# The branch to a fallback path, moved ahead of the last sums and stores of a two-stage kernel

## Chip, cores, metric

The kernel runs on one core of one Trainium2 chip. The metric is the device time of one execution in microseconds, as the median of several runs. The core has five engines with instruction streams of their own: TensorE (PE, and PEld for its weight loads), VectorE (DVE), ScalarE (ACT), GpSimd (POOL) and SyncE (SP), which here only starts transfers.

## What is computed

Two stages follow each other: a gated linear recurrence for each of 4 x 8 heads, and a bilinear feed-forward layer over the 3072 tokens that come out of it.

```python
f = 1 / (1 + exp(-f_logit))                      # q, k, v, f_logit: (4, 8, 768, 48)
for t in range(768):
    state = f[:, :, t, :, None] * state + k[:, :, t] (x) v[:, :, t]   # 48 x 48 for each head
    y[:, :, t] = q[:, :, t] @ state
x = y.transpose(0, 2, 1, 3).reshape(3072, 384)
out = ((x @ w_a) * (x @ w_b)) @ w_out            # w_a, w_b: (384, 1536), w_out: (1536, 384)
```

## The kernel before

There are two complete ways to the output in one program. `by_quotients` is the fast one. It divides running products of the gates by each other, which holds only while the decays stay within a range. `by_levels` is general and slower. The fast way always runs. On the way it gathers evidence on the range (`tails`, `held`), near its end `sum_held` and `check_held` (L915 to L927) turn it into one integer `bad`, and after it the program reads `bad` (`values_load`, L129) and branches (L130): if it is set, `convert_again` and `by_levels` do all the work once more, else nothing is left to do. With the inputs of the reference it is not set. A `values_load` is an instruction on each of the five engines (TENSOR_LOAD in the profile), and so is the branch (COMPARE_BRANCH). On the side that is not taken, each engine adds to its semaphores what the other side would have added: these are the EVENT_SEMAPHORE rows of L130. The end block, with the line of the launch, L1619, waits for every semaphore on SyncE and then brings all engines together.

The fast way works in 8 blocks of 384 tokens. The recurrence of a block (scores, masked products, carried state) comes in two units of four heads. Its result goes by DMA into `xT`, the layer's input with channels on partitions. The up products of blocks 0 and 1 are plain (`up_steps`, L593). Those of the other six use a scheme with 15 products of half size in place of 18 (`up_triples`, products L715, sums L707), with sums of weights made beforehand in `combine_w_ba`. The products with `w_out` (`down`, from L790) take two groups of 128 tokens at a time and use a scheme with 7 block products in place of 8. Each block product is six matmuls of 128x192 outputs (L808).

The order of work is made at build time. `main` (from L1103) is the list of TensorE's steps, with the copies and sums that belong to them standing behind the product that they follow; other work (`lines`, L1145) is fitted in by a planner with costs and due times, `fill` at L1236. At the end of `main` only steps of `down` for the last pair of groups are left, and the instructions stand in the order in which `down` yields them. That order, for this pair, is

1. products `x0` (L849), ACT copies it to `u2` (L823)
2. products `m1` (L854), ACT copies them into half of `o1` (L830)
3. products added to `x0` (L856), ACT copies it into half of `o0` (L834); a sum for `s4` on VectorE (L859)
4. products `x1` (L860), then `sum_u2` and `sum_u3` on VectorE (L837, L840)
5. products `m0` (L863), then `last_of(1, 1, m0)`, a sum on VectorE (L843)
6. products added to `x1` (L865), then `last_of(1, 0, x1)` and `store(1)` (L847), a DMA of 128 x 384 numbers that SyncE starts
7. products added to `m0` (L868), then `last_of(0, 1, m0)` and `store(0)`

`u2`, `o1` and `o0` are tiles from rotating pools, in SBUF; `x0`, `m1`, `x1` and `m0` are the four banks `ps_f` in PSUM.

Of the kernel before, what the change touches and what calls it, by code (L numbers as in the profile page):

```python
# [12 lines left out]
FP32 = mybir.dt.float32  # L13
# [9 lines left out]
BLK = 384  # L23
# [74 lines left out]
@with_exitstack  # L98
def kernel(
    ctx: ExitStack,  # L100
    tc: tile.TileContext,
    q: bass.AP,
    k: bass.AP,
    f_logit: bass.AP,
    v: bass.AP,
    masks: bass.AP,
    moe_w_a: bass.AP,
    moe_w_b: bass.AP,
    moe_w_out: bass.AP,
    out: bass.AP,  # L110
):
    nc = tc.nc
    DFF, DM = moe_w_out.shape[0], out.shape[1]
    NKT, NFT = DM // 128, DFF // 128

    const = ctx.enter_context(tc.tile_pool(name="const", bufs=1))

    def fixed(shape, name, dtype=FP32):
        return const.tile(shape, dtype, tag=name, name=name)

    ident = fixed([128, 128], "ident")
    w_ba = fixed([128, 2, NKT, DFF], "w_ba")
    w_out = fixed([128, NFT, DM], "w_out")
    bad = fixed([1, 1], "bad", I32)
    weights = (w_ba, w_out)

    with ExitStack() as pools:
        by_quotients(pools, tc, q, k, f_logit, v, moe_w_a, moe_w_b, moe_w_out, out, ident, weights, bad)
    again = nc.values_load(bad[0:1, 0:1], min_val=0, max_val=1, skip_runtime_bounds_check_because="it is a comparison's result")  # L129
    with tc.If(again > 0):  # L130
        with ExitStack() as pools:
            convert_again(pools, tc, weight_pieces(*weights, moe_w_a, moe_w_b, moe_w_out))
        with ExitStack() as pools:
            by_levels(pools, tc, q, k, f_logit, v, masks, out, ident, weights)


def by_quotients(ctx, tc, q, k, f_logit, v, moe_w_a, moe_w_b, moe_w_out, out, ident, weights, bad):
    nc = tc.nc
    B, H, D, S = q.shape
    w_ba, w_out = weights  # L140
# [207 lines left out]
            yield  # L348

    ps_x, ps_y = (ps_a.tile([128, 2, 512], FP32, tag=n, name=n) for n in ("ps_x", "ps_y"))  # L350
    ps_f = [ps_a.tile([128, 512], FP32, tag=f"ps_f{i}", name=f"ps_f{i}") for i in range(4)]
    idle = list(range(4))

    def tokens(n, c, p):
# [221 lines left out]
    def on(engine, load, due, do, *args, copied=False):  # L576
        return engine + COPIED * copied, load, beats[0] + due if due else 1 << 30, do, *args
# [209 lines left out]

    down_first = [thirds[0]]

    def down(pair):  # L790

        b11, b21, b22 = (w_out[:, HFT * i:HFT * i + HFT, HM * j:HM * j + HM] for i, j in ((0, 0), (1, 0), (1, 1)))
        t1, t2, t3, t4 = combos
        (blk0, g0), (blk1, g1) = pair
        a11, a12 = (half_of(products(blk0)[:, g0], i) for i in range(2))
        a21, a22 = (half_of(products(blk1)[:, g1], i) for i in range(2))
        got = {}

        def block():
            down_first[0] = thirds[(thirds.index(down_first[0]) + 1) % 3]  # L800
            return thirds[thirds.index(down_first[0]) - 1].rearrange("p (k j t) -> p k j t", k=NI, j=2)

        def add(due, to, x, y, op=ALU.add):
            return on(DVE, 880, due, add_steps, to, x, y, op)

        def emit(to, x, w, start, i):
            for i in (i, i + 1):
                nc.tensor.matmul(  # L808
                    to, lhsT=x[:, i // 2, i % 2], rhs=w[:, NI * (i % 2) + i // 2],
                    start=start and i == 0, stop=i == HFT - 1, skip_group_check=True,  # L810
                )

        def times(to, x, w, start=False):
            for i in range(0, HFT, 2):
                yield on_pe(BEAT, emit, to, x, w, start, i)

        s3 = block()
        yield add(4, s3, a11, a21, ALU.subtract)
        x0, m1, x1, m0 = (ps_f[i][:, 0:HM] for i in free)

        def begin():
            got["u2"] = sb2.tile([128, HM], FP32, tag="u2", name="u2")
            nc.scalar.copy(got["u2"], x0)  # L823

        def part(i, j):
            return got["o", i][:, HM * j:HM * j + HM]

        def second():
            got["o", 1] = sb1.tile([128, DM], FP32, tag="o1", name="o1")
            nc.scalar.copy(part(1, 0), m1)  # L830

        def third():
            got["o", 0] = sb1.tile([128, DM], FP32, tag="o0", name="o0")
            nc.scalar.copy(part(0, 0), x0)  # L834

        def sum_u2():
            nc.vector.tensor_tensor(got["u2"], x1, got["u2"], ALU.add)  # L837

        def sum_u3():
            nc.vector.tensor_tensor(part(1, 0), got["u2"], part(1, 0), ALU.add)  # L840

        def last_of(i, j, x):
            nc.vector.tensor_tensor(part(i, j), x, got["u2"] if i == 0 else part(1, 0), ALU.add)  # L843

        def store(i):
            blk, g = pair[i]
            nc.sync.dma_start(out=out[blk * BLK + g * 128:blk * BLK + g * 128 + 128], in_=got["o", i])  # L847

        yield from times(x0, a11, b11, True)  # L849
        yield on(ACT, 220, 4, begin)  # L850
        s1, s2 = block(), block()
        yield add(10, s1, a21, a22)
        yield add(7, s2, s1, a11, ALU.subtract)
        yield from times(m1, s3, t3, True)  # L854
        yield on(ACT, 220, 7, second)
        yield from times(x0, a12, b21)  # L856
        yield on(ACT, 220, 7, third)
        s4 = block()
        yield add(10, s4, a12, s2, ALU.subtract)  # L859
        yield from times(x1, s2, t2, True)  # L860
        yield on(DVE, 270, 4, sum_u2)
        yield on(DVE, 270, 0, sum_u3)
        yield from times(m0, s1, t1, True)  # L863
        yield on(DVE, 270, 4, last_of, 1, 1, m0)
        yield from times(x1, a22, t4, True)  # L865
        yield on(DVE, 270, 8, last_of, 1, 0, x1)
        yield on(SP, ISSUE, 3, store, 1)
        yield from times(m0, s4, b22)  # L868
        yield on(DVE, 270, 4, last_of, 0, 1, m0)
        yield on(SP, ISSUE, 3, store, 0)  # L870

    def core_parts(s):

# [49 lines left out]
    def check_held():  # L923

        ps = ps_x[0:1, 0, 0:1]
        nc.tensor.matmul(ps, lhsT=some[:, 0:1], rhs=ones, start=True, stop=True)
        nc.vector.tensor_scalar(bad, ps, 128.0 * NU * 3, None, ALU.is_lt)  # L927

    def patterns():
        make_identity(nc, ident)  # L930
# [7 lines left out]
    with tc.manual_schedule():  # L938
# [161 lines left out]


        w_out_sums, (w_before, w_over) = list(combine_w_out()), combine_w_ba()
        main, beside, behind = [], {}, {}  # L1103
        for blk, i in ups[alone:]:
            main.extend(up_steps(blk, i))
            main.append(on(DVE, 480, 2, product))
# [2 lines left out]
        for blk in range(NBLK):  # L1109
            if blk >= 2:  # L1110
                beside[len(main)] = "x", blk
                main.extend(up_triples(blk))
                behind[blk] = len(main)
                ahead = 16
            b, odd = divmod(blk, 2)
            pairs = (((blk - 1, 0), (blk, 0)), ((blk, 1), (blk, 2))) if odd else (((blk, 1), (blk, 2)),)
            if blk == 1:
                pairs = (((0, 1), (0, 2)), *pairs)
            for two in pairs if blk else ():
                beside.setdefault(len(main), "out")  # L1120
                first, *steps = down(two)
                at = len(main) - ahead
                main.insert(at, first)
                beside = {n + (n > at): x for n, x in beside.items()}
                if blk == NBLK - 1 and two is pairs[0]:
                    steps.insert(0, on(DVE, 700, 0, sum_held))
                    steps.append(on(PE, 100, 0, check_held))
                main.extend(steps)
                behind.setdefault("down", len(main))
                ahead = 10  # L1130
# [141 lines left out]
        done = len(main)  # L1272
        for line in lines:
            emit_until(line, len(line.steps))


def by_levels(ctx, tc, q, k, f_logit, v, masks, out, ident, weights):


    nc = tc.nc  # L1280
# [13 lines left out]
    sb2 = ctx.enter_context(tc.tile_pool(name="sb2", bufs=2))  # L1294
    ab_pool = ctx.enter_context(tc.tile_pool(name="ab", bufs=NFT + 2))
    ps_a = ctx.enter_context(tc.tile_pool(name="ps_a", bufs=2, space=bass.MemoryType.PSUM))
    ps_f = ctx.enter_context(tc.tile_pool(name="ps_f", bufs=4, space=bass.MemoryType.PSUM))

    def fixed(shape, name):
        return fixedp.tile(shape, FP32, tag=name, name=name)  # L1300
# [219 lines left out]
    def ffn(b):  # L1520

        x = xT.pop(b)
        for blk in range(NB):
            cols = slice(blk * BLK, blk * BLK + BLK)
            ab = []
            for ft in range(NFT):
                ps = {}
                for nm, w in (("b", w_b), ("a", w_a)):
                    ps[nm] = ps_f.tile([128, 512], FP32, tag="f", name="f")[:, 0:BLK]
                    for kt in range(NKT):  # L1530
                        nc.tensor.matmul(
                            ps[nm],
# [8 lines left out]
                nc.vector.tensor_tensor(ab[ft], ps["a"], b_sb, ALU.mult)  # L1541
                yield
            for tg in range(NTG):
                o = ps_f.tile([128, 512], FP32, tag="f", name="f")[:, 0:DM]
                for ft in range(NFT):
                    y = ab[ft][:, tg * 128:tg * 128 + 128]
                    nc.tensor.matmul(o, lhsT=y, rhs=w_out[:, ft], start=ft == 0, stop=ft == NFT - 1)
# [75 lines left out]
```

## Time and profile before

| | |
|---|---|
| median of 3 runs | 598.5 us (598.17 to 599.41) |
| profiled execution | 597.91 us |
| its span, from the first to the last instruction | 596.2 us |
| mean granted clock of TensorE | 0.997 |
| chain that ended last, share of the span | PE 84%, DVE 10%, issue 2%, ACT 1%, DMA 1% |

The profile is of one execution. The 1.7 us between its time and its span lie outside the instructions. In rows of groups, "x12" counts instructions, and "mean ns" is the time of one. In the timeline each row is a start, a length, the engine and line, output <- input, and in brackets the idle time ahead of it with what ended it. A q behind an engine's name (SPq, PEldq) means its sequencer: reads of registers, branches, waits on semaphores and DMA issues, which do not count as busy. In views by line, three durations are the shortest, median and longest, and then come the first and last start. The page's chain ends like this in the order of time (start, length, what):

```profile
569.88 6.01 PE ps_f L808 x37
575.89 0.12 PE ps_x L926 x2
576.01 13.86 PE ps_f L808 x84
589.87 0.02 issue
589.89 0.36 DVE o L843
```

It ends with the last sum. What the program does after that (stores, reads of the flag, branches, waits) is sequencer work, which this chain does not follow.

### The profile page before, as it was taken

Reading aid. Unit: us, or ns where it says so; the run is one execution under the profiler, and the core shown is the slowest. Engines: PE = TensorE matmul, PEld = TensorE weight load, DVE = VectorE, ACT = ScalarE, POOL = GpSimd, SP = SyncE. Lnnn points to the kernel's source line nnn. Section 1 sums busy time; section 2 is a strip of 40 time slices with the busy share of each in tenths; the row PEclk is TensorE's granted clock in tenths of the full one; section 3 lists DMA queues with packets and bytes.
Section 4 is the critical chain, followed back from the end, with each engine's and each line's share of the span. In section 5 each row is a group of like instructions: output and inputs, shape, how many; then the busy total and the mean of one; then the engine's idle time right before and its main releaser. Section 6 shows DMA issues by size and latency. Waiting matters only on the chain.

```text
span 596.2 us, 13953 instructions
## 1 busy us (share of the span) xinstructions
PE 571.8 (96%) x5802; PEld 512.0 (86%) x5802; DVE 412.3 (69%) x786; ACT 269.3 (45%) x507; POOL 77.0 (13%) x71
## 2 busy tenths in 40 slices
PE   3899999999999999999999999999999999999995
PEld 1655655567999999999999999999999999999995
DVE  6899445599977778958895677838784256745741
ACT  6589959743123464245521354325431345144300
POOL 6254525354000000000000000000000000000000
PEclk9999999999999999999999999999999999999998
DMA  8697699099542440044004400050001100000000
GB/s 215 184 257 226 211 252 263 0 157 186 118 134 66 113 100 3 17 120 93 2 2 128 117 10 1 2 127 21 3 1 47 48 1 0 2 27 1 0 30 32
DMA packets 33273, 49.43 MB, mean 83 GB/s; under 512 B 3952, under 2 KB 24976, under 8 KB 33200
## 3 DMA queue, kind: packets, MB, share of 16 engines
q1 hardware_dynamic: 30000, 42.38, 26.0%
q0 software_dynamic: 3056, 5.92, 5.8%
q8 instruction: 47, 0.77, 0.6%
q14 instruction: 26, 0.21, 0.1%
q10 hardware_dynamic: 144, 0.15, 0.1%
HBM read 33.23 MB, written 4.72 MB: 64 GB/s over the span
## 4 chain that ended last, share of the span: by engine, by line
PE 84%; DVE 10%; issue 2%; ACT 1%; DMA 1%; SPq 0%; DVEq 0%; ACTq 0%
PE ps_f L715 35%; PE ps_f L808 28%; PE ps_f L593 13%; PE ps_y L484 2%; DVE inv L329 2%; PE ps_y L510 2%; PE ps_x L387 2%; PE ps_x L435 1%; PE ps_x L411 1%; DVE sums L707 1%; DVE groups L707 1%; DVE spare L329 1%; DVE f_in L316 1%; DVE q_in L333 1%; DVE w_ba L73 1%
## 5 line engine op out<-in xcount | busy, mean ns | idle before, releaser
L593 PE MATMUL ps_f<-xT,w_ba 128*128 128x384 f32 x288 | 95.6, 489 | 1.9 <-DMA xT<-y 1.4
L1271 ACT COPY sums<-ps_f 128x384 f32<-128x384 f32 x120 | 57.5, 480 | 75.9 <-PE ps_f L715 68.2
L593 PEld LDWEIGHTS ps_f<-xT,w_ba 128*128 128x128 f32 x288 | 53.9, 190 | 38.6 <-issue 2.6
L1271 ACT COPY groups<-ps_f 128x384 f32<-128x384 f32 x120 | 57.7, 481 | 62.9 <-PE ps_f L715 39.9
L715 PE MATMUL ps_f<-xT,w_ba 128*128 128x192 f32 x384 | 78.4, 327 | 0.0
L715 PEld LDWEIGHTS ps_f<-xT,w_ba 128*128 128x128 f32 x384 | 64.7, 190 | 0.2
L715 PE MATMUL ps_f<-groups,w_ba 128*128 128x192 f32 x288 | 55.5, 328 | 0.0
L715 PE MATMUL ps_f<-x_sums,raw 128*128 128x192 f32 x288 | 54.0, 331 | 1.2 <-DVE groups L707 0.9
L808 PE MATMUL ps_f<-w_out,sums 128*128 128x192 f32 x288 | 52.2, 329 | 0.3 <-DVE groups L615 0.3
L808 PE MATMUL ps_f<-w_out,groups 128*128 128x192 f32 x288 | 51.7, 328 | 0.0
L715 PEld LDWEIGHTS ps_f<-x_sums,raw 128*128 128x128 f32 x288 | 46.9, 190 | 4.3 <-DVE groups L707 1.8
L808 PE MATMUL ps_f<-spare,sums 128*128 128x192 f32 x288 | 49.0, 326 | 0.0
L715 PEld LDWEIGHTS ps_f<-groups,w_ba 128*128 128x128 f32 x288 | 47.8, 190 | 0.5 <-ACT groups L1271 0.3
L808 PEld LDWEIGHTS ps_f<-w_out,sums 128*128 128x128 f32 x288 | 47.1, 190 | 1.3 <-DVE groups L615 0.6
L808 PEld LDWEIGHTS ps_f<-w_out,groups 128*128 128x128 f32 x288 | 47.1, 190 | 0.7
L312 POOL TENSOR_SCALAR inv<-inv 128x768 f32<-128x768 f32 x14 | 13.1, 935 | 267.3 <-ACT inv L309 267.2
L808 PEld LDWEIGHTS ps_f<-spare,sums 128*128 128x128 f32 x288 | 47.1, 190 | 0.1
L60 POOL TENSOR_SCALAR sums<-sums 128x768 f32<-128x768 f32 (+1 forms) x20 | 39.7, 1983 | 45.0 <-ACT sums L58 44.8
L707 DVE TENSOR_TENSOR sums<-sums,groups 128x768 f32<-128x768 f32 x36 | 34.7, 965 | 14.2 <-ACT groups L1271 13.7
L707 DVE TENSOR_TENSOR sums<-ps_f,sums 128x384 f32<-128x384 f32 x60 | 32.9, 553 | 16.5 <-PE ps_f L715 15.0
L715 PE MATMUL ps_f<-x_sums,w_ba 128*128 128x192 f32 x192 | 39.3, 327 | 0.5 <-DVE sums L707 0.5
L715 PE MATMUL ps_f<-xT,raw 128*128 128x192 f32 x192 | 39.4, 328 | 0.0
(136 smaller groups left out, 868.0 us busy)
## 6 DMA issues: line engine op xcount, KB each, us to landing
raw<-w_ba POOLq DMA_DIRECT2D x11, 512.0 KB, 8.5
k_in<-in_k_dram SPq DMA_DIRECT2D x32, 144.0 KB, 3.8
q_in<-in_q_dram SPq DMA_DIRECT2D x32, 144.0 KB, 4.2
v_in<-in_v_dram SPq DMA_DIRECT2D x16, 288.0 KB, 5.4
raw<-in_moe_w_out_dram SPq DMA_DIRECT2D x6, 768.0 KB, 6.3
out_dram<-o SPq DMA_DIRECT2D x24, 192.0 KB, 1.9
f_in<-in_f_logit_dram SPq DMA_DIRECT2D x28, 144.0 KB, 2.9
xT<-y SPq DMA_DIRECT2D x45, 72.0 KB, 2.2
```

Source lines behind the costliest of these rows:

```text
L60: nc.gpsimd.tensor_scalar(h, h, HI_MAX, None, ALU.min)
L73: nc.vector.tensor_tensor(dst[:, rows], hu[:, rows], bit[:, rows], ALU.add)
L312: nc.gpsimd.tensor_scalar(inv, inv, EXP_K, 1.0, ALU.mult, ALU.add)
L329: nc.vector.tensor_tensor_scan(inv[:, w], inv[:, w], none[:, 0:C], first, ALU.mult, ALU.add)
L387: nc.tensor.matmul(ps[h][SUB * p:SUB * p + SUB, o:o + SUB], lhsT=kf[r, tokens(n, c, p)], rhs=qf[r, tokens(n, c, p)], start=True, stop=True,)
L484: nc.tensor.matmul(ps[p][e:e + D, o:o + SUB], lhsT=t["v"][r, n, c, h * D:h * D + D], rhs=at[r, h, o:o + SUB], start=o == 0, stop=True, ski ...
L510: nc.tensor.matmul(ps[p][e:e + D, o:o + SUB], lhsT=st[j][r, n], rhs=qf[r, tokens(n, c, p)], start=False, stop=True, skip_group_check=True,)
L593: nc.tensor.matmul(ps[nm][:, 0:BLK], lhsT=w[:, kt, ft * 128:ft * 128 + 128], rhs=xT[blk][:, kt], start=kt == 0, stop=kt == NKT - 1,)
L707: nc.vector.tensor_tensor(to, x, y, op)
L715: nc.tensor.matmul(ps[:, g], lhsT=sums_of_w[name][:, g, 128 * j:128 * j + 128], rhs=sums_of_x[blk][name], start=start and g == 0, stop=Tru ...
L808: nc.tensor.matmul(to, lhsT=x[:, i // 2, i % 2], rhs=w[:, NI * (i % 2) + i // 2], start=start and i == 0, stop=i == HFT - 1, skip_group_ch ...
L1271: do(*args)
```

## The change

The last two sums (`last_of(1, 0, x1)` and `last_of(0, 1, m0)`) and the two stores behind them leave the common stream. `down` puts them on a list, `ending`, and the program emits them in the other arm of the branch, so that they run when the flag is not set; if it is set, the general path writes all of the output, these rows too. The read of the flag moves into `down`, behind the sum for `s4` and ahead of the products `x1`, as a step of SyncE with a cost of 600 ns for the planner; as before it is an instruction on all five engines. The branch stands behind the last products on TensorE, behind `last_of(1, 1, m0)` on VectorE, behind the copy of `o0` on ACT, behind the read on SyncE and POOL. In this last pair `u2`, `o1` and `o0` lie in parts of `w_ba`, since the pools of the fast way are closed where the other arm begins. The four banks `ps_f` come from a pool of the whole program for the same reason, and `by_levels` uses them in rotation.

```diff
+    ps_f = ctx.enter_context(tc.tile_pool(name="ps_f", bufs=1, space=bass.MemoryType.PSUM))
+    banks = [ps_f.tile([128, 512], FP32, tag=f"ps_f{i}", name=f"ps_f{i}") for i in range(4)]
 
     with ExitStack() as pools:
-        by_quotients(pools, tc, q, k, f_logit, v, moe_w_a, moe_w_b, moe_w_out, out, ident, weights, bad)
-    again = nc.values_load(bad[0:1, 0:1], min_val=0, max_val=1, skip_runtime_bounds_check_because="it is a comparison's result")
-    with tc.If(again > 0):
+        again, ending = by_quotients(pools, tc, q, k, f_logit, v, moe_w_a, moe_w_b, moe_w_out, out, ident, weights, bad, banks)
+    with tc.If(again > 0) as general:
         with ExitStack() as pools:
             convert_again(pools, tc, weight_pieces(*weights, moe_w_a, moe_w_b, moe_w_out))
         with ExitStack() as pools:
-            by_levels(pools, tc, q, k, f_logit, v, masks, out, ident, weights)
+            by_levels(pools, tc, q, k, f_logit, v, masks, out, ident, weights, banks)
+
+    with general.Else():
+        with tc.manual_schedule():
+            for do, *args in ending:
+                do(*args)
...
-    def down(pair):
+    def down(pair, ending=None):
+        new = {}
+        if ending is not None:
+            new = {"u2": w_ba[:, 0, 0, 0:HM], "o1": w_ba[:, 0, 1, 0:DM], "o0": w_ba[:, 0, 2, 0:DM]}
+
+        def tile_of(pool, name, width):
+            return new[name] if new else pool.tile([128, width], FP32, tag=name, name=name)
...
         s4 = block()
         yield add(10, s4, a12, s2, ALU.subtract)
+        if ending is not None:
+            yield on(SP, 600, 0, read_bad)
         yield from times(x1, s2, t2, True)
         yield on(DVE, 270, 4, sum_u2)
         yield on(DVE, 270, 0, sum_u3)
+
+        def finish(due, i, *of):
+            if ending is None:
+                yield on(DVE, 270, due, last_of, i, *of)
+                yield on(SP, ISSUE, 3, store, i)
+            else:
+                ending.extend(((last_of, i, *of), (store, i)))
+
         yield from times(m0, s1, t1, True)
         yield on(DVE, 270, 4, last_of, 1, 1, m0)
         yield from times(x1, a22, t4, True)
-        yield on(DVE, 270, 8, last_of, 1, 0, x1)
-        yield on(SP, ISSUE, 3, store, 1)
+        yield from finish(8, 1, 0, x1)
         yield from times(m0, s4, b22)
-        yield on(DVE, 270, 4, last_of, 0, 1, m0)
-        yield on(SP, ISSUE, 3, store, 0)
+        yield from finish(4, 0, 1, m0)
...
+    again = []
+
+    def read_bad():
+        again.append(nc.values_load(
+            bad[0:1, 0:1], min_val=0, max_val=1, skip_runtime_bounds_check_because="it is a comparison's result"
+        ))
...
-                first, *steps = down(two)
+                first, *steps = down(two, ending if blk == NBLK - 1 and two is pairs[-1] else None)
```

More of the change, by code (lines that the diff above doesn't have):

```diff
@@ L133, with by_quotients @@
         with ExitStack() as pools:
-            by_levels(pools, tc, q, k, f_logit, v, masks, out, ident, weights)
-def by_quotients(ctx, tc, q, k, f_logit, v, moe_w_a, moe_w_b, moe_w_out, out, ident, weights, bad):
+            by_levels(pools, tc, q, k, f_logit, v, masks, out, ident, weights, banks)
[3 more added lines that the diff above has]
+                do(*args)
+def by_quotients(ctx, tc, q, k, f_logit, v, moe_w_a, moe_w_b, moe_w_out, out, ident, weights, bad, ps_f):
     nc = tc.nc
@@ L350, in by_quotients @@
     ps_x, ps_y = (ps_a.tile([128, 2, 512], FP32, tag=n, name=n) for n in ("ps_x", "ps_y"))
-    ps_f = [ps_a.tile([128, 512], FP32, tag=f"ps_f{i}", name=f"ps_f{i}") for i in range(4)]
     idle = list(range(4))
@@ L821, in begin @@
         def begin():
-            got["u2"] = sb2.tile([128, HM], FP32, tag="u2", name="u2")
+            got["u2"] = tile_of(sb2, "u2", HM)
             nc.scalar.copy(got["u2"], x0)
@@ L828, in second @@
         def second():
-            got["o", 1] = sb1.tile([128, DM], FP32, tag="o1", name="o1")
+            got["o", 1] = tile_of(sb1, "o1", DM)
             nc.scalar.copy(part(1, 0), m1)
         def third():
-            got["o", 0] = sb1.tile([128, DM], FP32, tag="o0", name="o0")
+            got["o", 0] = tile_of(sb1, "o0", DM)
             nc.scalar.copy(part(0, 0), x0)
@@ L1102, in by_quotients @@
         w_out_sums, (w_before, w_over) = list(combine_w_out()), combine_w_ba()
-        main, beside, behind = [], {}, {}
+        main, beside, behind, ending = [], {}, {}, []
         for blk, i in ups[alone:]:
@@ L1274, in by_quotients, with by_levels @@
             emit_until(line, len(line.steps))
-def by_levels(ctx, tc, q, k, f_logit, v, masks, out, ident, weights):
+    return again[0], ending
+def by_levels(ctx, tc, q, k, f_logit, v, masks, out, ident, weights, banks):
     nc = tc.nc
@@ L1296, in by_levels @@
     ps_a = ctx.enter_context(tc.tile_pool(name="ps_a", bufs=2, space=bass.MemoryType.PSUM))
-    ps_f = ctx.enter_context(tc.tile_pool(name="ps_f", bufs=4, space=bass.MemoryType.PSUM))
+    banks = itertools.cycle(banks)
     def fixed(shape, name):
@@ L1528, in ffn @@
                 for nm, w in (("b", w_b), ("a", w_a)):
-                    ps[nm] = ps_f.tile([128, 512], FP32, tag="f", name="f")[:, 0:BLK]
+                    ps[nm] = next(banks)[:, 0:BLK]
                     for kt in range(NKT):
@@ L1543, in ffn @@
             for tg in range(NTG):
-                o = ps_f.tile([128, 512], FP32, tag="f", name="f")[:, 0:DM]
+                o = next(banks)[:, 0:DM]
                 for ft in range(NFT):
```

## The prediction

> **What bounds the kernel now.** I read the page first: which engine fills the span, and where it is empty.
>
> ```profile
> span 596.2 us, 13953 instructions
> PE 571.8 (96%) x5802; PEld 512.0 (86%) x5802; DVE 412.3 (69%) x786; ACT 269.3 (45%) x507; POOL 77.0 (13%) x71
> ```
>
> TensorE bounds it all but at the two ends. The change touches only the last 20 us, so next comes the table of busy times by stretch (columns: PE, PEld, DVE, ACT, POOL, clock, DMA share, GB/s).
>
> ```profile
> 582.00:590.30 8.30, 7.86 (x49) 7.56 (x47) 1.79 (x5) 0.32 (x1) 0.00 (x0) 1.00 0.08 28
> 590.30:596.20 5.90, 0.00 (x0) 0.00 (x0) 0.00 (x0) 0.00 (x0) 0.00 (x0) 0.66 0.13 42
> ```
>
> The last 5.9 us hold no arithmetic at all. This tail bounds what the change can give. The timeline shows what leads into it:
>
> ```profile
> 587.74 2.11 PE L808 MATMUL ps_f<-w_out,sums 128*128 128x192 f32 x12
> 587.94 0.36 DVE L843 TENSOR_TENSOR o<-ps_f,o 128x192 f32<-128x192 f32 x1 [1.59 <-PE ps_f L808]
> 588.33 2.32 SPq L847 DMA_DIRECT2D out_dram<-o  x2
> 589.89 0.36 DVE L843 TENSOR_TENSOR o<-ps_f,u 128x192 f32<-128x192 f32 x1 [1.59 <-PE ps_f L808]
> ```
>
> The products end at 589.85, the last sum runs 589.89 to 590.25, SyncE starts the last store at 590.3. Then the views by source line, for the read of the flag (L129) and the branch (L130):
>
> ```profile
> L129 POOLq TENSOR_LOAD <-bad x1: 491/491/491, 576.4 to 576.4; - x1
> L129 ACTq TENSOR_LOAD <-bad x1: 481/481/481, 582.2 to 582.2; - x1
> L129 PEldq TENSOR_LOAD <-bad x1: 491/491/491, 586.8 to 586.8; - x1
> L129 DVEq TENSOR_LOAD <-bad x1: 542/542/542, 589.9 to 589.9; - x1
> L129 SPq TENSOR_LOAD <-bad x1: 535/535/535, 590.7 to 590.7; - x1
> ```
>
> ```profile
> L130 SPq EVENT_SEMAPHORE  x8: 17/17/17, 594.0 to 594.5; - x8
> L130 POOLq COMPARE_BRANCH  x1: 54/54/54, 576.9 to 576.9; - x1
> L130 POOLq EVENT_SEMAPHORE  x1: 17/17/17, 579.8 to 579.8; - x1
> L130 ACTq COMPARE_BRANCH  x1: 54/54/54, 582.7 to 582.7; - x1
> L130 ACTq EVENT_SEMAPHORE  x1: 17/17/17, 585.2 to 585.2; - x1
> L130 PEldq COMPARE_BRANCH  x1: 3322/3322/3322, 587.4 to 587.4; - x1
> L130 DVEq COMPARE_BRANCH  x1: 72/72/72, 590.5 to 590.5; - x1
> L130 PEldq EVENT_SEMAPHORE  x1: 51/51/51, 590.8 to 590.8; - x1
> L130 SPq COMPARE_BRANCH  x1: 50/50/50, 591.3 to 591.3; - x1
> L130 DVEq EVENT_SEMAPHORE  x1: 21/21/21, 593.8 to 593.8; - x1
> ```
>
> Each engine reads the flag and branches for itself, and between the branch and its next instruction lie, to the hundredth in the trace's records, 2.46 us (ACT), 2.66 (SP), 2.84 (POOL), 3.23 (DVE) and 3.38 (PE). SyncE does its round after the last store, so it is back only at 594.0. Last, how long stores take (view of L847) and which queues moved packets from 591.3 to 594.1:
>
> ```profile
> DMA to landing us min/median/max: 1.8/1.9/3.7
> ```
>
> ```profile
> q8 instruction: 1, 0.02, 3.2%
> q14 instruction: 2, 0.02, 1.7%
> ```
>
> By the trace's issue and landing records the 3.7 is the last store's own: issued 590.3, landed 594.03. In the packet records 15 of the 16 DMA engines finish their eight packets by 591.9. The sixteenth starts at 592.78, where the 16 KB instruction packet of q8 (591.36, 1.42 us) ends. So two things end together at 594.0: SyncE's refill and a store held up by a fetch.
>
> [...]
>
> **The change part by part.** In the built programs the order of instructions is the same on every engine up to the last pair of token groups, and there the reads, branches, two sums and two stores do stand where the diff puts them. `bad` is written at 576.33, so no read waits for it.
>
> *SyncE.* Its read and branch leave the tail. They now follow the store of 576.6 (issue over by 577.0): read to 577.6, refill to about 580.3. Nothing is queued behind until the stores at 588.3. In the tail this removes 590.7 to 594.0 from SyncE, but of that only what the landing does not cover counts.
>
> *VectorE.* The read follows the sum of 580.14, before a stretch idle to 584.1: 0.54 us, hidden. The branch follows `last_of(1, 1, m0)`, which starts at 585.99; sequencers run on once an instruction starts (the old read began 0.01 us after the last sum's start). Branch at 586.0, 3.23 us to its next instruction, so at 589.3 the first sum of the other arm: 1.35 us later than its 587.94 now. It ends at 589.65. The last sum waits for the products until 589.89 anyway, so cover remains, though only 0.24 us; beyond that every delay reaches the end in full. Bounds: ACT's 2.46 leaves 0.9 us of cover; a refill of 4 would cost 0.5. I take no cost. Store 1 moves from 588.3 to about 589.7; SyncE issues in 0.33 us and is free for the last store at 590.3.
>
> *TensorE.* The read now stands ahead of the `x1` products. Its sequencer ran 3 us ahead at the end (read at 586.8, products to 589.85). Ahead of `x1` it is held until the copy of `x0` ends at 578.5, while products run from 578 to 582. So some 0.5 us of read is hidden; bounds 0 and 0.5, I take 0 (the move cannot itself gain, as the products set the pace). At the end the read is gone from in front of the branch, which comes 0.6 us earlier, 586.8.
>
> *ACT, POOL.* Same places, same times. Three ACT copies write into `w_ba` rather than fresh tiles; its last readers are the L715 products, over by 562.3, so no wait is added; the waits for stores of the old tiles go, but the copies started when the products ended, so nothing is gained. The banks' new pool and the general path's use of them do not run.
>
> *The end of SyncE.* In the new order six of the balancing waits stand before the landing is awaited, and the end block waits for it in sixth place. These cost 0.06 to 0.07 us each, 10 of them some 0.7 us, beside the landing. What follows it is the end block from its sixth wait. That block's SyncE waits begin at 594.6 now:
>
> ```profile
> L1619 SPq EVENT_SEMAPHORE  x14: 17/28/28, 594.6 to 596.1; - x14
> ```
>
> The sixth starts at 594.88, so 1.3 us follow to 596.19; today 2.15 us follow the landing.
>
> *The landing itself.* Last store at 590.3 as now, for its sum waits for the products. The new end is 590.3 + landing + 1.34. Of 24 stores, those that met no fetch took 1.84 to 1.95 us. Three met a 16 KB fetch: begun 0.01 us after the issue, 2.24; 0.93 after, 3.64; 1.05 after, 3.72 (this one). That fetch is TensorE's second page, begun 0.6 us after it resumes (591.36 against 590.76). With its branch 0.6 earlier I put it at 590.8 to 591.0, 0.45 to 0.7 after the issue: between those rows, so 2.4 to 3.4; I take 2.9. Sum: 590.3 + 2.9 + 1.34 = 594.55, against 596.19: **1.6 us less**. The profiled execution took 597.91 (span 596.19 and 1.7 around it), 0.6 under the median of 598.5; the difference carries over: 596.3 profiled, **596.9 us** as a median.
>
> **Rivals.**
> 1. *The fetch misses the last store.* Landing 1.9, end 593.55, 2.65 less: 595.9. For it: three stores with a fetch 0.5 to 0.9 us ahead took 1.89 to 2.08. Against: the fetch would have to begin at 589.9, 0.9 us sooner than I put it.
> 2. *The transfer is late anyway.* If TensorE resumes only when its last products have drained, its second fetch stays at 591.36 and the landing at 3.7: end 595.35, 0.8 less: 597.7. For it: TensorE alone records the branch itself as 3.3 us long. Against: its 16 KB packet starts 0.95 us after the branch and ends 1.5 us before it resumes, as on VectorE.
> 3. *VectorE's refill becomes the bound, and the kernel is slower.* [...] two refills stand one after the other: 586.0 + 6.5 = 592.5 for the first sum, 0.8 for both sums, store at 593.3, landing at 2.9, 1.34: end 597.5, 1.3 more: 599.8. It decides from a first sum at about 591.1, 5.1 us after the branch. For it: the sums now stand behind a refill, with 0.24 us to spare. [...]
>
> **How the numbers follow.** Forecast 0.50, rival 1 0.20, rival 2 0.22, rival 3 0.08. The runs before lie from 0.3 below to 0.9 above their median, so less than 0.2% (1.2 us) can't be told from no change. Forecast: 0.40 faster, 0.10 same; rival 1: 0.20 faster; rival 2: 0.04 faster, 0.18 same; rival 3: 0.02 same, 0.06 slower. Range: rival 1 less 0.5 for the runs, 595.4; rival 2 plus 0.6, 598.3; rival 3 is left out.
>
> **What would show it.** The SyncE flag read near 577; VectorE's first other-arm sum near 589.3 and its last still at 589.9; the last store issued at 590.3; TensorE idle nowhere between 578 and 582; the 16 KB packet at 590.8 to 591.0; the landing near 2.9; 1.3 us from landing to end. I am wrong if the last sum starts later than 589.9, or if the landing stays at 3.7.

## The result, and the profile after

The kernel takes **596.81 us** (median of 17 runs, 595.8 to 598.16) against 598.43 before (17 runs, 597.78 to 599.41): ratio 0.9973, 95% interval 0.9965 to 0.998, so 1.2 to 2.1 us less. 596.9 was predicted. The profiled execution took 596.65. Its page begins

```profile
span 594.9 us, 13948 instructions
```

594.93 to the hundredth, where 594.55 was predicted. The table of busy times by stretch, cut where the products end (columns as before):

```profile
582.00:589.90 7.90, 7.90 (x49) 7.61 (x47) 1.43 (x4) 0.32 (x1) 0.00 (x0) 1.00 0.03 7
589.90:594.93 5.03, 0.00 (x1) 0.00 (x0) 0.36 (x1) 0.00 (x0) 0.00 (x0) 0.98 0.24 81
```

TensorE stays full to 589.90, where it was done at 589.86 before. So all of the difference lies in the tail: 5.03 us from the end of the last product to the end of the span, 6.33 before. The timeline ahead of it:

```profile
587.79 2.11 PE L822 MATMUL ps_f<-w_out,sums 128*128 128x192 f32 x12
589.09 0.36 DVE L857 TENSOR_TENSOR w_ba<-ps_f,w_ba 128x192 f32<-128x192 f32 x1 [2.69 <-issue]
589.47 1.23 SPq L861 DMA_DIRECT2D out_dram<-w_ba  x2
589.94 0.36 DVE L857 TENSOR_TENSOR w_ba<-ps_f,w_ba 128x192 f32<-128x192 f32 x1 [0.50 <-PE ps_f L822]
```

The first sum of the other arm now waits for "issue" and no longer for products: this is VectorE's refill, the time from its branch (586.06) to its next instruction (588.99): 2.93 us, in which two 8 KB instruction packets move on q14, at 586.69 and 587.09. The last sum still waits for TensorE, and VectorE sits idle for 0.50 us ahead of it: that is the cover that was left, the further delay that this wait would still have hidden. Reads (L955) and branches (L131) by source line:

```profile
L955 SPq TENSOR_LOAD <-bad x1: 535/535/535, 577.1 to 577.1; - x1
L955 PEldq TENSOR_LOAD <-bad x1: 488/488/488, 579.0 to 579.0; - x1
```

```profile
L131 SPq EVENT_SEMAPHORE  x6: 17/17/17, 590.7 to 591.1; - x6
...
L131 SPq COMPARE_BRANCH  x1: 50/50/50, 577.7 to 577.7; - x1
...
L131 DVEq COMPARE_BRANCH  x1: 72/72/72, 586.1 to 586.1; - x1
...
L131 PEldq COMPARE_BRANCH  x1: 3438/3438/3438, 586.8 to 586.8; - x1
L131 PEldq EVENT_SEMAPHORE  x1: 51/51/51, 590.3 to 590.3; - x1
```

SyncE has branched 13 us ahead of its last store and does its balancing waits at 590.7 to 591.1, beside the landing. TensorE's branch comes at 586.84 and it resumes at 590.34, still inside the tail. One 16 KB packet of q8 starts in that gap, at 587.76, and a second at 590.93. What that does to the last store is seen in the DMA view from 590.3 to 593.7 (slices of 0.085 us; busy tenths, then GB/s):

```profile
DMA  7999985900269979820000101010100000000000
GB/s 289 343 361 434 361 325 181 211 0 0 108 253 398 361 289 398 289 73 0 0 0 0 18 0 18 0 18 0 18 0 36 18 18 0 0 0 0 0 0 0
...
q8 instruction: 1, 0.02, 2.4%
...
out_dram<-w_ba SPq DMA_DIRECT2D x1, 192.0 KB, 3.2
```

The first hump belongs to the store ahead of it, the second, over by 591.85, to the last store. Then nothing moves for four slices, and then eight packets trickle by one at a time (18 GB/s over 0.085 us is one packet of 1.5 KB). The packet records don't name the engine, but by their times these are the last store's eight on the one DMA engine that carried the 16 KB instruction packet of q8, from 590.93 to 592.24: the first of them starts at 592.23, when fifteen of the store's sixteen parts have landed. The sixteenth, and with it the store, lands at 593.61. The end block follows:

```profile
L1650 SPq EVENT_SEMAPHORE  x16: 17/28/28, 580.5 to 594.9; - x16
```

Two of these sixteen are balancing waits that now stand among the stores, at 580.45 and 589.85. By the records five of the end block's own are over at 591.46, the sixth goes through at 593.63, when the store has landed, and the span ends 1.32 us after the landing. Before, it ended 2.15 after. There SyncE came back from its branch only at 593.97, and its second balancing wait, on the semaphore of the last store, went through at 594.06, 0.03 after the landing; the other six and the whole end block came behind that. From there to the sixth wait of the end block took 0.82 us, and this work now runs beside the landing. The sum: last store issued 0.05 later (590.37), landing 0.48 shorter (3.24 against 3.72), end 0.83 sooner after it: 1.26 less.

### The profile page after: what moved, and what is told of

Its sections match the earlier page's. It is cut to its first block, busy times and chain, and to the rows that moved or that the text cites. A ratio compares the mean times of both kernels' runs of the same rounds, so it can differ in the third digit from the quotient of the medians.

```text
span 594.9 us, 13948 instructions
## 1 busy us (share of the span) xinstructions
PE 573.2 (96%) x5802; PEld 513.2 (86%) x5802; DVE 411.9 (69%) x786; ACT 268.9 (45%) x507; POOL 77.6 (13%) x71
## 4 chain that ended last, share of the span: by engine, by line
PE 84%; DVE 11%; issue 2%; ACT 1%; DMA 1%; SPq 0%; DVEq 0%; ACTq 0%
PE ps_f L720 35%; PE ps_f L822 28%; PE ps_f L598 13%; PE ps_y L489 2%; DVE inv L335 2%; PE ps_y L515 2%; PE ps_x L392 2%; PE ps_x L440 1%; PE ps_x L416 1%; DVE sums L712 1%; DVE f_in L322 1%; DVE groups L712 1%; DVE st L469 1%; DVE q_in L339 1%; DVE spare L335 1%
```

## The experiments

The theory: SyncE's refill and the landing held up by TensorE's fetch bound the end of the kernel before, side by side; the change takes away the first and shortens the second. The rivals: the early read alone brings the gain; the late landing alone was the bound; where TensorE branches has no price. Here are the tails of all profiles, in us. "Fetch" is the start of TensorE's second 16 KB packet (q8 is taken as TensorE's by its times: in the kernel after one packet starts 0.92 behind its branch and one 0.59 behind its resuming, and no_branch shows none from 590.1 on), counted from the start of the last store's issue, and how long it took; "landing" runs from there to the last of the store's sixteen completions; "tail" runs from the end of the last product of the kernel's own (an added 1x1 product is not counted) to the end of the span.

| kernel | median (runs), ratio [95%] | fetch | landing | landing to end | tail |
|---|---|---|---|---|---|
| before | 598.43 (17) | +1.05, 1.42 | 3.72 | 2.15 | 6.33 |
| after | 596.81 (17), 0.9973 [0.9965, 0.998] | +0.56, 1.31 | 3.24 | 1.32 | 5.03 |
| after_again | 597.63 (1) | +0.90, 1.36 | 3.43 | 1.31 | 5.21 |
| after_third | 596.66 (1) | +0.66, 1.49 | 3.51 | 1.31 | 5.29 |
| read_early | 598.2 (13), 0.9999 [0.999, 1.0007] | +0.46, 0.96 | 2.78 | 2.52 | 5.75 |
| branch_only | 596.97 (16), 0.9977 [0.997, 0.9985] | +1.69, 0.88 | 1.96 | 1.32 | 3.90 |
| branch_only_again | 595.59 (1) | +1.61, 0.90 | 1.96 | 1.31 | 4.17 |
| before_pe_late | 598.51 (21), 1.0001 [0.9995, 1.0008] | +3.21, 1.39 | 2.37 | 3.81 | 6.63 |
| pe_late | 595.67 (5), 0.9958 [0.9945, 0.9972] | +2.48, 0.93 | 2.39 | 1.32 | 4.17 |
| no_branch | 595.74 (5), 0.9955 [0.9942, 0.9968] | none | 1.86 | 1.28 | 3.60 |
| products_in_arm | 596.39 (6), 0.9967 [0.9955, 0.9979] | -2.16, 1.02 | 1.84 | 1.31 | 3.63 |
| dve_late | 597.83 (22), 0.9989 [0.9981, 0.9997] | -0.30, 1.03 | 2.61 | 1.31 | 5.20 |
| dve_late_again | 598.03 (1) | +0.03, 1.54 | 3.40 | 1.31 | 5.99 |
| pe_late_split | 595.86 (5), 0.9955 [0.9942, 0.9968] | +2.03, 1.20 | 2.15 | 1.25 | 3.83 |

The runs were timed in groups. The kernel before took 598.34 to 598.54 as a median in the three larger ones, so medians of different groups compare to about 0.2 us.

Spans of single profiles aren't compared: in some executions all the work stands later by a constant. TensorE's 1000th instruction into `ps_f` starts at 257.97 in the kernel before and 1.16 later in read_early, and the last one, at 589.53 before, is 1.16 later too. The shift arises long before any edit, and the tail leaves it out.

**read_early: the early read, without the other arm.** The tiles of the last pair come from the rotating pools again; the banks stay in the pool of the whole program. The rest of the edit, against the kernel after:

```diff
-    with general.Else():
-        with tc.manual_schedule():
-            for do, *args in ending:
-                do(*args)
...
         def finish(due, i, *of):
-            if ending is None:
-                yield on(DVE, 270, due, last_of, i, *of)
-                yield on(SP, ISSUE, 3, store, i)
-            else:
-                ending.extend(((last_of, i, *of), (store, i)))
+            yield on(DVE, 270, due, last_of, i, *of)
+            yield on(SP, ISSUE, 3, store, i)
```

> The flag is read early, as in the changed kernel, but the last sums and stores stay in the common stream and the branch stands behind them. My theory (the end is store issue + landing + the waits that SyncE still has to pass): SyncE stores at 590.3, branches at once, is back from its refill at 593.4; TensorE branches 0.5 us earlier than before, so its second fetch still meets the store, landing 3.2 us, 593.6; then the long row of waits as before, 2.1 us: span 595.7, 0.5 us less than before (596.2). Rival A (the early read is what counts, not where the branch stands): the whole gain, span 594.9, 1.3 less.

No gain that can be measured, though the interval reaches 0.6 us of one; the tail of the one profile is 0.58 shorter. The branches by line:

```profile
L131 SPq EVENT_SEMAPHORE  x8: 17/17/17, 594.5 to 595.1; - x8
...
L131 SPq COMPARE_BRANCH  x1: 50/50/50, 591.9 to 591.9; - x1
```

The landing is early (2.78, over by 594.25), but SyncE branches behind the last store and is back only at 594.54. The early read does not explain a gain of 1.2 to 2.1 us, and neither does the pool of the banks, which this kernel has too.

**branch_only: the other arm, with the read where it was.** Against the kernel after:

```diff
         yield add(10, s4, a12, s2, ALU.subtract)
-        if ending is not None:
-            yield on(SP, 600, 0, read_bad)
...
         yield from finish(4, 0, 1, m0)
+        if ending is not None:
+            yield on(SP, 600, 0, read_bad)
```

> The sums and stores stand in the other arm as in the changed kernel, but the flag is read only at the end of the common stream, ahead of the branch. My theory: VectorE's read of 0.54 us now stands ahead of its branch, so its first sum starts near 589.65, the last sum ends 590.4, the store starts at 590.45; TensorE's read puts its second 16 KB fetch 0.5 later, to 591.4, 0.95 us after the store's issue, so the landing is 3.6 to 3.7 us, and 1.3 us follow: span 595.4, 0.8 less than before and 0.5 more than the changed kernel. Rival A (only the early read counts): 596.2, no gain. Rival B (the landing has nothing to do with the fetch's time): landing as in the changed kernel, 595.0.

> Sums and stores in the other arm, the flag read at the end of the common stream, once more. Its first profile had TensorE's refill at 3.9 us instead of 3.4, the second fetch 1.69 us after the store's issue and a landing of 1.96. My theory: with a refill of 3.4 us the fetch begins near 0.9 us after the issue and the landing is 3.5; with 3.9 it is 1.9 again. From the last product to the end 5.4 or 3.9 us.

The other arm alone brings 0.9 to 1.8 us: about what the whole change brings. For SyncE it brings the early read along, for with the stores in the other arm nothing is left to stand ahead of its read:

```profile
L954 SPq TENSOR_LOAD <-bad x1: 531/531/531, 577.3 to 577.3; - x1
```

So what this kernel takes back is the early read on VectorE and TensorE alone. The landing I had wrong. TensorE branches at 587.65, 0.6 later than in the kernel after once the 0.2 by which this execution stands later is taken off, and takes 3.95 us to resume (3.50 there). So its fetch begins 1.69 after the store's issue, behind the last of the store's packets (which starts 1.54 after it), and no longer holds the store up:

```profile
L131 PEldq EVENT_SEMAPHORE  x1: 51/51/51, 591.6 to 591.6; - x1
```

Both profiles show this, but both are of executions 1.2 to 1.4 us below the median of 596.97; what the others look like no trace shows. The late read has a price too: VectorE reads the flag between `last_of(1, 1, m0)` and its branch, so the first sum of the arm starts at 589.84, the two stores crowd together, and SyncE, which issues the first until 590.55 and then has two waits to go through, starts the last at 590.75, 0.58 behind the start of the last sum (0.43 in the kernel after).

**before_pe_late: TensorE held back, in the kernel before.** ScalarE copies one number of `x1`, and a 1x1 product behind TensorE's last products waits for that copy, so that its sequencer cannot run ahead to the branch:

```diff
+        def late_copy():
+            nc.scalar.copy(w_ba[0:1, 1, 1, 0:1], x1[0:1, 0:1])
+
+        def late_product():
+            nc.tensor.matmul(ps_x[0:1, 0, 0:1], lhsT=w_ba[0:1, 1, 1, 0:1], rhs=ones[0:1], start=True, stop=True)
...
         yield on(SP, ISSUE, 3, store, 1)
+        if late:
+            yield on(ACT, 220, 0, late_copy)
         yield from times(m0, s4, b22)
+        if late:
+            yield on_pe(100, late_product)
```

> The kernel before, with the same holding back of TensorE's branch by one copy and one 1x1 product. My theory: the landing falls to 1.9 us (592.2), but SyncE is still in its refill until 594.0, so the end stays: span 596.1, no difference (within 0.1 us). Rival C (before, the late landing alone bounded the end): 1.8 us less, 594.3. Rival B: landing 3.7 as before, 596.2.

TensorE's branch moved from 587.38 to 589.26 and the landing fell to 2.37, over by 592.81. It did not reach 1.9, as TensorE's first 16 KB packet now began 0.01 us after the store's issue; the store landed 1.37 after that packet's end. The time did not move, for SyncE's own round is still there:

```profile
L130 SPq EVENT_SEMAPHORE  x8: 17/17/17, 594.4 to 594.9; - x8
...
L130 SPq COMPARE_BRANCH  x1: 50/50/50, 591.4 to 591.4; - x1
```

So the late landing was not the only bound: shortened alone, it gives nothing.

**pe_late: the same two steps in the kernel after.**

```diff
         yield from finish(8, 1, 0, x1)
+        if ending is not None:
+            yield on(ACT, 220, 0, late_copy)
         yield from times(m0, s4, b22)
+        if ending is not None:
+            yield on_pe(100, late_product)
         yield from finish(4, 0, 1, m0)
```

> The changed kernel, with TensorE's branch held back: ScalarE copies one number of x1 after its last products, and one 1x1 product behind the last ones waits for that copy, so that TensorE's sequencer reaches the branch near 588.3 instead of 586.8. The output is unchanged. My theory: its first fetch ends by 590.3, before the last store's packets, its second begins near 592.4, after them; the landing falls to 1.9 us, and the span to 590.4 + 1.9 + 1.3 = 593.6: 1.3 less than the changed kernel although it does more. Rival B (the landing has nothing to do with TensorE's fetch): 594.9 or a little more.

Here it helps: 1.7 to 3.3 us less than before, 1.1 less than the kernel after by the medians, 0.9 to 1.1 less by the tails. There are five runs, and the two intervals against the kernel before just overlap; but of the 17 runs of the kernel after only two are as low as the highest of these five (596.17). Of its timeline:

```profile
588.12 0.15 ACT L864 COPY w_ba<-ps_f 1x1 f32<-1x1 f32 x1 [5.53 <-PE ps_f L822]
...
589.96 0.18 PE L867 MATMUL ps_x<-ones,w_ba 1*1 1x1 f32 x2
```

TensorE branches at 588.32, resumes at 592.38 and fetches at 592.98, when the store has landed (592.89). I expected more. The landing took 2.39 and not 1.9. Most of that lies in the issue itself, the longer of these two:

```profile
L861 SPq DMA_DIRECT2D out_dram<-w_ba x2: 332/492/652, 589.6 to 590.5; - x2
```

SyncE took 0.65 us to issue the last store, where it took 0.33 in the kernel after, and the store's packets begin 0.32 later than there. The store ahead was then still under way: it met TensorE's first 16 KB packet, which ended 0.28 us after this issue, and landed 2.50 after its own (1.86 in the kernel after). That this held the issue back is a reading of the times, not a test. Fifteen parts of the last store then land by 592.67 and the sixteenth at 592.89; an 8 KB packet on q14, by its time a fetch of ScalarE, which branches later as well (588.1, back at 590.9), began 1.03 after the issue and may account for that part.

**no_branch: the read, the branch and the general path left out.** Against the kernel before:

```diff
-    again = nc.values_load(bad[0:1, 0:1], min_val=0, max_val=1, skip_runtime_bounds_check_because="it is a comparison's result")
-    with tc.If(again > 0):
-        with ExitStack() as pools:
-            convert_again(pools, tc, weight_pieces(*weights, moe_w_a, moe_w_b, moe_w_out))
-        with ExitStack() as pools:
-            by_levels(pools, tc, q, k, f_logit, v, masks, out, ident, weights)
```

> The general path is left out, and with it the read of the flag and the branch: for inputs out of range this kernel would give wrong values. Spans have shifted as a whole by up to 1 us between executions, so I give the time from the last store's issue to the end (5.87 us before, 4.56 in the changed kernel). My theory (what the branch costs is TensorE's fetch in the landing and the waits behind it): no fetch, landing 1.9, then 1.3: 3.2 us, which is 1.35 less than the changed kernel and 2.65 less than before. Rival B (the late landing of the last store does not come from the fetch): landing 3.2, 4.5 us in all, as the changed kernel.

From the last store's issue to the end it took 3.14 us (3.2 expected). This is the floor, and pe_late stands within 0.1 us of it by the medians, though with five runs each the intervals reach 0.8 us to either side, and by the tails it stands 0.6 above. Of the 2.7 us that the branch cost before, the change recovers 1.6; most of the rest is the landing (3.24 against 1.86 here).

**products_in_arm: the last six products in the other arm too** (twelve instructions in the views).

```diff
         s4 = block()
+        if ending is not None:
+            s4 = w_ba[:, 1, 0, 0:PIECE].rearrange("p (k j t) -> p k j t", k=NI, j=2)
...
-        yield from times(m0, s4, b22)
+        if ending is None:
+            yield from times(m0, s4, b22)
+        else:
+            ending.extend((do, *args) for _, _, _, do, *args in times(m0, s4, b22))
```

> The changed kernel, with the last six products (those added to m0) in the other arm as well, their input s4 in a part of w_ba. My theory: TensorE branches near 585.2 and is back only 3.4 to 3.8 us later, near 588.8, while these products could have started at 587.9: 0.9 us of idle TensorE on the path. In return its second fetch is over before the last store, landing 1.9 instead of 3.2. From store to end 3.2 us, but the store 0.9 later: 0.4 us less than the changed kernel in all. Rival D (a refill under a running product queue is hidden): no idle, and 1.3 us less than the changed kernel.

Its timeline shows what an early branch on TensorE costs:

```profile
589.13 2.19 PE L822 MATMUL ps_f<-w_out,w_ba 128*128 128x192 f32 x12 [0.94 <-issue]
```

The row shows 0.94 us without products; with the partly filled end of the stretch ahead of it, the products end 1.18 later than in the kernel after, once the 0.24 by which this execution stands later is taken off. In return both of TensorE's 16 KB fetches are over by 590.64, ahead of the last store, and the landing takes 1.84 in place of 3.24. The two nearly cancel; the medians differ by 0.4 us, and the intervals overlap. Its tail of 3.63 starts from these later products and is not to be set beside the others.

**dve_late: VectorE's branch made later.** Four copies of 128x192, each reading what the one before it wrote, behind `last_of(1, 1, m0)`:

```diff
+        def copied_on(n):
+            x = part(1, 1) if n == 0 else w_ba[:, 1, 1, HM * n:HM * n + HM]
+            nc.vector.tensor_copy(w_ba[:, 1, 1, HM * n + HM:HM * n + 2 * HM], x)
...
         yield on(DVE, 270, 4, last_of, 1, 1, m0)
+        if ending is not None:
+            for n in range(4):
+                yield on(DVE, 270, 0, copied_on, n)
```

> The changed kernel, with four dependent copies of 128x192 on VectorE behind last_of(1, 1, m0), 0.4 us apart, so that its branch comes 1.6 us later. The output is unchanged. My theory: the first sum of the other arm at 590.6, the last sum ends 591.4, 1.1 us later, the store starts at 591.45. But TensorE's second fetch (590.9, 1.3 us) is then over when the store's packets start, so the landing falls to 1.9 to 2.2: the end within 0.3 us of the changed kernel (span 594.7 to 595.0). Rival B (the landing is late whatever the fetch does): landing 3.2, span 596.0, 1.1 more. Rival D (refill of VectorE hidden even so): no change in the last sum's time.

> The changed kernel with four dependent copies ahead of VectorE's branch, once more, since its timed runs were 1.0 us above the changed kernel's while its profile's tail (last product to end) was only 0.2 us longer. My theory in its first form: tail 5.0 to 5.3 us, with a fetch that begins before the store's issue and a landing of 1.9 to 2.6. If the landing does not gain from the later store: tail 6.0, with the landing at 3.2.

About 1.0 us worse than the kernel after by the medians: with the cover used up, VectorE's refill reaches the end. The last sum starts 0.64 and 0.63 us after the last product ends, where it was 0.04, and the two stores crowd together, so that the last is issued 1.28 us after that product in both (0.47 in the kernel after). A landing near 1.9 as the store moves behind the fetch did not come: the fetch began 0.30 ahead of the issue and 0.03 behind it, and the landing took 2.61 and 3.40. The two are late in different ways. In dve_late_again fifteen parts land by 1.86 after the issue and one at 3.40, as in the kernel after. In dve_late all sixteen land between 2.44 and 2.61, for SyncE needed 1.09 us for the issue:

```profile
L861 SPq DMA_DIRECT2D out_dram<-w_ba x2: 336/714/1092, 592.0 to 592.5; - x2
```

The store ahead of it had met the fetch there and landed 2.64 after its own issue. So this pair prices the delay of the store, and not a landing without a fetch.

**pe_late_split: the first half of the last store sent early, on top of pe_late.**

```diff
+        def store_half():
+            blk, g = pair[0]
+            nc.sync.dma_start(out=out[blk * BLK + g * 128:blk * BLK + g * 128 + 128, 0:HM], in_=part(0, 0))
...
+            yield on(SP, ISSUE, 0, store_half)
             yield on(SP, 600, 0, read_bad)
```

> The changed kernel with TensorE's branch held back as in pe_late, and the last store cut in two: the half of its columns that is ready at 582.5 is stored then, ahead of SyncE's read and branch, so that only 128 x 192 numbers are stored after the last sum. My theory: eight packets of 768 instead of 1536 bytes for each DMA engine after the last sum, landing 1.7 instead of 1.9 (2.4 in the profile of pe_late, where a small fetch met it): 0.2 us less than pe_late or nothing that can be measured, 2.7 less than before. If packets cost the same at half their size, no change against pe_late.

Only the other half of the columns is stored after the last sum. The landing was 2.15 against 2.39 in one profile each; the times show no difference from pe_late that can be measured.

**after_again, after_third: two more profiles of the kernel after.**

> The changed kernel once more, for one more profile. From the last product's end to the end of the span it was 5.03 us before. My theory: TensorE's second 16 KB fetch again begins 0.4 to 0.9 us after the last store's issue, and the landing lies at 2.4 to 3.5; if the fetch begins later than 1.2 us after the issue, the landing is 1.9. Rival B (landing and fetch are not tied): landings that do not follow the fetch's place.

> The changed kernel a third time, same expectations: a landing of 2.4 to 3.5 with the fetch begun 0.4 to 0.9 us after the last store's issue, 1.9 with a fetch begun over 1.2 us after it.

Landings of 3.43 and 3.51, and 1.31 from landing to end both times. So 3.24 was no outlier to the slow side.

## Why the prediction was right, step by step

- **SyncE** held in full: read at 577.1, balancing waits at 590.7 to 591.1, and 1.32 us from landing to end (1.34 predicted). That 1.25 to 1.32 appears in every kernel whose SyncE branches early, and 2.15 to 3.81 in all three that branch behind the last store. Read_early and before_pe_late show that this step is the condition for the gain: with SyncE's round still in the tail, landings of 2.78 and 2.37 brought no measurable time.
- **VectorE** held: branch at 586.06, first sum of the arm at 589.09 (589.3 predicted), last sum still at 589.94, as soon as the products allow. The cover was 0.50 us, not 0.24, as its refill took 2.93 and not 3.23. Dve_late shows that it was the only cover: pushed past it, the delay reaches the last sum.
- **TensorE's read** held: at 579.0, with TensorE busy for all 6.00 us from 576 to 582.
- **TensorE's branch and fetch** held: branch at 586.84 (586.8 predicted), 16 KB packet at 590.93 (590.8 to 591.0). Counted from the store's issue the packet began 0.56 after it, and 0.90 and 0.66 in the other two profiles, where 0.45 to 0.7 was predicted. Rival 2 has no support: TensorE resumes 0.4 us after its last product in after and after_third, 0.8 after it in after_again and 2.3 in pe_late, so the end of the products does not fix the time. In no profile does it resume before they end (0.3 after is the least, in read_early), so it isn't excluded that they can hold it back.
- **The landing was mis-sized.** It took 3.24, and 3.43 and 3.51 in the other two profiles, in place of 2.9. The failed step is the interpolation between stores by when their fetch began. What counts is when the fetch ends: in the three profiles of after the store lands 1.37, 1.16 and 1.36 us after the packet's end, in read_early 1.36, and the three stores of the kernel before from which the prediction interpolated land 1.36, 1.37 and 1.26 after it (for the last one the prediction's own text has both times, 592.78 and 594.03). A fetch at 590.8 to 591.0 that lasts 1.42, plus 1.26, gives a landing of 593.5 to 593.7, where 593.61 was measured. Taken so, the span is 594.8 to 595.0. The pair of dve_late, with two stores close together, has 1.88 and 1.83. That the fetch is the cause is shown by the four profiles in which it falls before or behind the last store's packets, or is left out: products_in_arm, branch_only twice and no_branch land after 1.84 to 1.96. The prediction gave this last range too narrowly: one of the 24 stores of the kernel before, issued at 471.2, met no fetch and took 2.09. Its sum does not rest on that.
- **The rivals.** Rival 1, a fetch that misses the last store, did not happen in the three profiles of the kernel after, but does in branch_only and pe_late, where the second fetch comes too late to meet it, and in products_in_arm, where it comes too early, as rival 1 had it. Rival 3, VectorE as the bound, needed a second refill behind the first, with a first sum at about 591.1; that sum started at 589.09, 3.03 us after the branch. Its 0.08 was my estimate: no run here tests what would bring a second refill.

The timed gain of 1.6 us (1.2 to 2.1) is somewhat more than the profiles show: their tails shrink by 1.0 to 1.3, and there is one profile of the kernel before. The near match of 596.9 and 596.81 owes something to that, as the landing was taken too short by 0.3 to 0.6: that much of it is luck.

What stays open: why TensorE takes 3.4 us from its branch to its next instruction in the kernel before, 3.5, 3.8 and 3.5 in the three profiles of after, and 3.8 to 4.1 in branch_only, before_pe_late and pe_late. The same code at another place in the program might tell; that was not tried. It matters, as these tenths decide whether the fetch meets the last store. Open too is what makes SyncE's issue of a store last 0.65 and 1.09 us in pe_late and dve_late.

## What to carry to other kernels

A branch is paid for by each engine on its own, in the time until that engine's next instruction (in the kernel after 2.75 us on SyncE, 2.93 on VectorE, 2.99 on GpSimd, 3.10 on ScalarE, 3.50 on TensorE), so put it where the engine has slack, and price what slack is left: here SyncE had 9 us (back at 580.45, next store at 589.47), VectorE 0.5 and TensorE, behind its last products, needs none (they end at 589.90, after its branch at 586.84). A refill is also a transfer (a 16 KB packet took 1.31 us in the kernel after), and seven stores that by their times shared a DMA engine with one landed 1.16 to 1.37 us after its end, when their own packets had followed; so count from the end of the fetch. When two things end together, shortening one may show nothing: before_pe_late took away the late landing alone, without effect. The reverse shows more here, since the change also moves SyncE's waits beside the landing: in after_third the landing was still 3.51, only 0.21 shorter than before, and the tail was 1.04 shorter.

## What the runs showed that was not expected

One 1x1 product that waits for a copy, more work for TensorE, makes the kernel 1.1 us faster by the medians (595.67 against 596.81): it keeps TensorE's sequencer from starting its second fetch into the last store (fetch at 592.98, store landed at 592.89). By the medians the whole branch, with a fallback path behind it, then costs nothing (595.67 against 595.74 without it), though the tails of the single profiles still differ by 0.6. And whole executions shift: in read_early, dve_late and pe_late_split TensorE stands 1.16, 1.38 and 1.55 us later than in the kernel before, by the same amount 258 us into the span and at its last product. The edits are not the cause, for dve_late_again, the same kernel as dve_late, stands 1.05 earlier than it. This is as large as the effect studied, and it is the reason for reading the tail and not the span.
